# Hash attention and maxout FFN on one core: later modelled landings in the kernel's own planner, earlier weight halves, and V casts moved to GpSimd

## The chip, the core and the metric

The kernel runs on one core of a Trainium2 chip, in one launch. The metric is device time in microseconds, the median of several runs. A profiled execution of the same program gives the span, the busy times and the trace. The engines are TensorE (PE, with its weight loads as PEld), VectorE (DVE), ScalarE (ACT), GpSimd (POOL) and SyncE (SP), which here only issues transfers. Each engine works through its instructions in the order in which they stand, and waits for semaphores of the others.

## What is computed

```python
# q, k, v: (4, 8, 768, 64) fp32; proj: (64, 6)
q_bits = einsum('bhsd,dk->bhsk', q, proj) > 0     # 6 bits: a bucket
k_bits = einsum('bhsd,dk->bhsk', k, proj) > 0
scores = where(q_bucket == k_bucket, q @ k.T / 8, -1e9)
attn = softmax(scores)                            # sum + 1e-9
x = (attn @ v) laid out as (3072, 512)
h = maximum(maximum(x @ w1, x @ w2), x @ w3)      # w: (512, 768)
out = h @ w_out                                   # (3072, 512) fp32
```

A query sees only keys of its own bucket. The kernel does not mask: the bits are appended to q and k as six more rows of the contraction, with a weight so large that a key which differs in one bit vanishes in the exponential.

## The kernel before

**Tiling.** The 8 heads of each of the 4 batches are handled in pairs, so there are 16 pairs, written (b, pr) below. For one pair q, k and v are loaded by three transfers of SP (`load`, L245), into four buffers each. `split_h` and `split_r` (L259, L270) make an fp16 part and an fp16 remainder. Both are transposed, on TensorE for the first six pairs (`pe_T`, L288, evacuated by `evac_T`), and by a DMA transpose on SP for the others (`xbar`, L281). `hash_mm` (L299) multiplies by the projection; `hash_bits0` or `hash_bits` (L314, L327) compares with zero. The bits then make a trip: `bit_T` transposes them on TensorE, `bit_evac` copies them on DVE, `bit_out` (L347) writes them to DRAM and `bit_in` (L351) reads them into their rows of the operand `T`. This trip is called the bounce. Up to the third pair, `hash_mm` adds the product of the high and the low half of the projection in PSUM, by 48 matmuls; from the fourth on it makes both halves side by side by 24 matmuls, and DVE compares them by two instructions in place of one.

**V.** `vcast` (L355) casts V to fp16 into `vone`, which holds a batch and has two copies. From batch 1 on, `vsum` (L359, three GpSimd instructions) sums V over the chunks, and `mean_mm` (L368) gives the column mean by one matmul; for batch 0 it takes six matmuls of the cast V itself. The mean stands in for a query that meets no key. The cast runs on GpSimd for batches 0 and 1, and on ACT for batches 2 and 3.

**Attention.** The work of a pair is cut into 12 units, numbered through u = 0 to 191. A unit is a `score` (L389, two matmuls of 384 columns into one of two `sc` buffers), an `expo` on ACT (L399) and an `attend` (L404, six matmuls of 65 columns). Six units make a block, which has the one `av` bank until `norm_t` (L419) on DVE has read it; `norm_x` divides. All blocks of batch 0 come first (u = 0 to 47). From batch 1 on, the pairs of the first half of the queries come before those of the second: pair (1,0) starts at u = 48, (1,1) at 54, (1,2) at 60, (1,3) at 66, and (2,0) at 96.

**FFN.** When a half of a batch is normalized, `x_bar` (L456), a DMA transpose on SP, turns it. 18 `l1` (L473, four matmuls each) make six blocks of the hidden layer from three weight matrices; `l1_evac` takes the maximum on DVE, the first of three also on ACT. Three `l2` (L492, six matmuls of 512 columns) give the output rows, evacuated by `l2_evac` into `osb` buffers and sent by `store` (L504) on SP. An `l1` needs its weight half: (0,0), (0,1), (0,2) are the first halves of the three matrices, (1,0), (1,1), (1,2) the second. All six come by GpSimd transfers that cast on the way (`load_w`, L538), behind a small wait instruction `hold` (L645) for the second halves. The output weights come by SP as fp32 into two `ws` buffers (`stage_w`, L659) and are cast on GpSimd (`cast_w`, L665).

**What sets the order.** The pools, tiles and semaphores take the order of the program, and the program is written by a planner. `Plan.run` (L46) simulates the engines when the program is built: each task has an engine or a choice of two with a duration, a priority, dependencies, and counts of buffers that it takes and gives. At each modelled moment a free engine takes the ready task of the smallest priority number. A transfer is modelled as an issue on its engine, a place in one common queue for its `xfer` time, and then a fixed POST of 1.2 us until it counts as landed. The order that results is emitted; at run time each engine keeps it, however long things really take. So a change of a modelled landing changes no instruction by itself. It changes which tasks were thought ready, and thereby the order on all engines.

`mm` names three PSUM banks which `pe_T`, `hash_mm`, `bit_T`, `mean_mm`, `l1` and `l2` share, each until its evacuation.

Of the kernel before, what the change touches and what calls it, by code (L numbers as in the profile page):

```python
# [16 lines left out]


class Task:
    def __init__(self, kinds, prio, deps, emit, take=(), give=(), after=(), lat=0.0, xfer=0.0, hold=0.0):  # L20
        self.kinds, self.prio, self.emit = kinds, prio, emit
        self.deps = [d for d in deps if d is not None]
        self.take, self.give, self.lat, self.xfer, self.hold = take, give, lat, xfer, hold
        self.after = [t for t in after if t is not None]
        self.start = None


class Plan:
# [17 lines left out]
    def run(self):  # L46
        users, left = {}, {}
        for n, t in enumerate(self.tasks):
            t.n = n
            left[t] = len(t.deps)  # L50
            for d in t.deps:
                users.setdefault(d, []).append(t)
        ready = {t for t in self.tasks if not left[t]}
        engines = sorted({k[0] for t in self.tasks for k in t.kinds})
        busy = dict.fromkeys(engines, 0.0)
        queue = []
        now, events, n = 0.0, [], 0
        while n < len(self.tasks):
            moved = True
            while moved:  # L60
                moved = False
                for e in engines:
                    if busy[e] > now:
                        continue
                    best = None
                    for t in ready:
                        dur = dict(t.kinds).get(e)
                        if dur is None or any(self.free[r] <= 0 for r in t.take) or any(
                                x.start is None for x in t.after):
                            continue  # L70
                        if best is None or (t.prio, t.n) < (best[0].prio, best[0].n):
                            best = t, dur
                    if best is None:
                        if e == "PE" and self.filler and self.filler(now):
                            busy[e] = now + 0.1
                            events.append((busy[e], -1, None))
                            moved = True
                        continue
                    t, dur = best
                    ready.discard(t)  # L80
                    for r in t.take:
                        self.free[r] -= 1
                    busy[e] = now + dur
                    t.start, t.engine = now, e
                    if t.hold:
                        busy[e] = 1e9
                        events.append((now + dur, -2, t))
                    else:
                        events.append((busy[e], -1, None))
                    if t.hold:  # L90
                        pass
                    elif t.xfer:
                        events.append((busy[e] + PRE_DMA.get(e, 0.3), -2, t))
                    else:
                        events.append((now + dur + (t.lat or self.LAT[e]), t.n, t))
                    if t.emit:
                        t.emit(e)
                    n += 1
                    moved = True
            events.sort(key=lambda x: x[:2])  # L100
            if not events and not queue:
                stuck = [(t.kinds, t.prio, [r for r in t.take if self.free[r] <= 0])
                         for t in sorted(ready, key=lambda t: t.prio)]
                raise RuntimeError(f"plan stuck: {n} of {len(self.tasks)} at {now}, {self.free}: {stuck[:12]}")
            then = min(now + queue[0][0] if queue else 1e9, events[0][0] if events else 1e9)
            if queue:
                queue[0][0] -= then - now
            now = then
            while queue and queue[0][0] < 1e-6:
                t, hold = queue.pop(0)[1:]  # L110
                if hold:
                    busy[t.engine] = now
                    queue.insert(0, [t.xfer - t.hold, t, 0.0])
                    continue
                events.append((now + POST, t.n, t))
            events.sort(key=lambda x: x[:2])
            while events and events[0][0] <= now:
                at, kind, t = events.pop(0)
                if kind == -2:
                    queue.append([t.hold or t.xfer, t, t.hold])  # L120
                    continue
                if t is None:
                    continue
                for r in t.give:
                    self.free[r] += 1
                for x in users.get(t, ()):
                    left[x] -= 1
                    if not left[x]:
                        ready.add(x)
        self.end = now  # L130
# [3 lines left out]
def kernel(  # L134
# [36 lines left out]
    XT = 4  # L171
    HT = 13
    XN = 2
    OSB = 4

    konst = ctx.enter_context(tc.tile_pool(name="konst", bufs=1))
    raw = ctx.enter_context(tc.tile_pool(name="raw", bufs=4))
# [120 lines left out]

    def hash_mm(b, pr, heads, e):  # L299
        hps = bank(("h", b, pr), "hps")  # L300
        summed = 4 * b + pr < 3
        K = NBITS if summed else 2 * NBITS
        for n in range(2):
            for hh in range(*heads):
                for c in range(NCH):
                    a = n * NA2 + hh * NCH + c
                    o = hps[:, a * K : (a + 1) * K]
                    if summed:
                        for i in range(2):
                            nc.tensor.matmul(o, T[b, pr][:, a, :], PAB[:, i * K : (i + 1) * K], start=i == 0, stop=i == 1)  # L310
                    else:
                        nc.tensor.matmul(o, T[b, pr][:, a, :], PAB[:], start=True, stop=True)  # L312
# [42 lines left out]
    def vcast(b, pr, e):  # L355
        copy(e, vones[b % 2][:, 2 * pr : 2 * pr + 2, :, 0:D],
             raws["v", b, pr][:].rearrange("p h (c d) -> p h c d", d=D))
# [190 lines left out]
    def value(b, pr, dep):  # L548
        U = first_unit[b, pr]
        prev = at_last.get((b - 2, pr))  # L550
        if b == 0:
            ready_v[b, pr] = add(("POOL", 0.85), U - 6, [dep, prev], lambda e: vcast(b, pr, e), give=("v",))
            vs = ready_v[b, pr]
        else:
            ready_v[b, pr] = add(("POOL", 0.9) if b == 1 else ("ACT", 0.72), U - 6, [dep, prev], lambda e: vcast(b, pr, e))
            vs = add(("POOL", 2.0), U - 5, [dep, ready_v[b, pr], ready_m.get((b if pr > 1 else b - 1, (pr + 2) % 4))],
                     lambda e: vsum(b, pr, e), give=("v",))
        m = add(("PE", 0.34 if b == 0 else 0.06), U - 3, [vs], lambda e: mean_mm(b, pr, e), take=("mm",))
        ready_m[b, pr] = add(("DVE", 0.28), U - 3, [m], lambda e: mean_evac(b, pr, e), give=("mm",))

    def prep(b, pr):
# [3 lines left out]
        if b > 0:  # L565
            for n in "qkv":
                g = divmod(4 * b + pr - GATE, 4)
                if b == 1:
                    g = {("q", 0): (0, 2), ("k", 0): (0, 2)}.get((n, pr), (0, 3) if pr < 3 else (1, 0))
                loads[n, b, pr, (0, 2)] = add(("SP", 0.5), U - 44 + 0.1 * "qkv".index(n), [],  # L570
                                              lambda e, n=n: load(n, b, pr, (0, 2), e), take=(n,), xfer=1.1,
                                              after=[last_load[0], bounced[g], xbars.get(4 * b + pr - 2)])
                last_load[0] = loads[n, b, pr, (0, 2)]
        value(b, pr, loads["v", b, pr, (0, 2)])
# [42 lines left out]
                                  give=("mm",)))  # L617
            both_rs += rs
        if not by_pe:
            ev = [add(("SP", 0.6), p0 + 2, both_rs, lambda e: xbar(b, pr, e), xfer=4.6, hold=3.4, take=("T",))]  # L620
            xbars[4 * b + pr] = ev[0]
        plan.join(ev, ("s",))
        hm = add(("PE", 1.3 if 4 * b + pr < 3 else 0.67), p0 + 4, ev + [mp], lambda e: hash_mm(b, pr, (0, 2), e), take=("mm",))
        hb = add(("DVE", 0.3 if 4 * b + pr < 3 else 0.62), p0 + 5, [hm],
                 (lambda e: hash_bits(b, pr, e)) if 4 * b + pr >= 3 else (lambda e: hash_bits0(pr, (0, 2), e)), take=("bit",), give=("mm",))
        bT = add(("PE", 0.11), p0 + 6, [hb], lambda e: bit_T(b, pr, e), take=("mm",), give=("bit",))
        be = add(("DVE", 0.28), p0 + 6, [bT], lambda e: bit_evac(b, pr, e), take=("bt",), give=("mm",))
        bo = add(("SP", 0.65), p0 + 7, [be], lambda e: bit_out(b, pr, e), take=("dr",), give=("bt",), xfer=0.05,
                 after=[last_copy[0]])
        bi = add(("SP", 0.65), p0 + 7, [bo], lambda e: bit_in(b, pr, e), give=("dr",), xfer=0.25)  # L630
        bounced[b, pr] = last_copy[0] = bi
        if b == 0 and pr < NP - 1:
            for hh in range(2):
# [12 lines left out]
        t = small.tile([P, 1], FP16, tag="hold", name="hold")  # L646
        nc.gpsimd.tensor_copy(t[D : D + NBITS, :], T[b, pr][D : D + NBITS, NA - 1, P - 1 : P])

    plain = ()
    wst_tiles = {}  # L650

    def w_view(w, i):
# [15 lines left out]
    def weights(b, pr, parts):  # L668
        if (pr or b) and parts[0] not in plain and parts[0] != "o":
            prev = add(("POOL", 0.1), -150, [bounced[b, pr]], lambda e: hold(b, pr, e), after=[wprev[0]])  # L670
        elif pr or b:
            prev = bounced[b, pr]
        else:
            prev = ready_v[0, 1]
        for w in parts:
            if w == "o" or w in plain:
                parts = []
# [128 lines left out]
```

## Time and profile before

| | us |
|---|---|
| median of 7 runs | 274.04 |
| lowest and highest of them | 272.57, 277.96 |
| the profiled execution | 275.18 |
| its span | 273.4 |
| busy: PE, DVE, ACT, POOL | 257.9, 177.3, 196.1, 47.5 |

The profiled execution is 1.8 us longer than the span of its engines. The granted clock of TensorE was 0.999 over the span. The page's second part cuts the span into 40 slices of 6.8 us; a digit is the busy share of a slice in tenths. The engines' busy sums are union times of instructions; a matmul counts up to its modelled end, which lies after the start of the next one, so that a gap shorter than that does not show in this row.

A line of the timeline has the start, the time taken, the engine, the line of the kernel, the operation and its tiles, and in brackets how long the engine had stood idle before it and what ended that. A line of the waits has the engine, its line, what it waited for, and then the total, the number of times and the longest.

### The profile page before, as it was taken

How to read it: one execution, taken by the hardware profiler on the slowest of the kernel's cores; microseconds unless marked ns; L12 is line 12 of the kernel's file. 1: busy time of each engine (PE TensorE's matmuls, PEld its weight loads, DVE VectorE, ACT ScalarE, POOL GpSimd, SP SyncE). 2: the span in 40 equal slices, each digit the busy share in tenths (PEclk: the TensorE clock that was granted, in tenths of full speed). 3: DMA queues.
4: the chain of work that ended last, by engine and by line, in shares of the span. 5: the costliest groups of instructions: out<-in, count | busy, mean ns of one | idle time of the engine just before them, and what ended most of it. 6: DMA issues, size and time to landing. Idle time of an engine off the chain costs nothing.

```text
span 273.4 us, 7378 instructions
## 1 busy us (share of the span) xinstructions
PE 257.9 (94%) x3016; PEld 175.7 (64%) x3016; DVE 177.3 (65%) x389; ACT 196.1 (72%) x283; POOL 47.5 (17%) x61
## 2 busy tenths in 40 slices
PE   8799996699999899979999999999999999999995
PEld 8688675467656566656666667666566656555552
DVE  4898698897767698386789735565246525445250
ACT  4798997689838789868988988899889432232322
POOL 1180075753303222030330300000000000000000
PEclk9999999999999999999999999999999999999999
DMA  6996499699995979869995783300510041020303
GB/s 199 370 213 101 136 309 217 192 201 320 224 243 182 288 215 167 197 216 215 206 242 187 143 192 90 68 2 2 134 41 1 15 121 41 6 111 2 115 0 116
DMA packets 67392, 41.30 MB, mean 151 GB/s; under 512 B 48030, under 2 KB 63646, under 8 KB 67358
## 3 DMA queue, kind: packets, MB, share of 16 engines
q1 hardware_dynamic: 64110, 38.47, 54.2%
q0 software_dynamic: 3168, 2.36, 6.1%
q8 instruction: 23, 0.38, 0.6%
q14 instruction: 11, 0.09, 0.1%
q10 hardware_dynamic: 80, 0.00, 0.0%
HBM read 25.72 MB, written 6.84 MB: 119 GB/s over the span
## 4 chain that ended last, share of the span: by engine, by line
PE 71%; DMA 12%; DVE 7%; SPq 3%; POOL 2%; issue 2%; ACT 2%; ACTq 0%; POOLq 0%
PE ps L478 31%; PE sc L395 16%; PE po L496 9%; PE av L413 9%; DMA v<-in_v_dram 7%; DMA q<-in_q_dram 4%; DVE s L273 2%; SPq L250 2%; DVE s L268 2%; PE hps L312 1%; ACT AT L401 1%; PE tps L292 1%; DMA T<-dr 1%; POOL vt L363 1%; PE hps L310 1%
## 5 line engine op out<-in xcount | busy, mean ns | idle before, releaser
L401 ACT ACTIVATE AT<-sc 128x768 f16<-128x768 f32 x192 | 146.2, 812 | 20.3 <-PE sc L395 19.3
L478 PE MATMUL ps<-xT,w_sb 128*128 128x384 f16 x576 | 106.3, 326 | 0.3 <-DVE ht L204 0.3
L395 PE MATMUL sc<-T 128*128 128x384 f16 x384 | 93.2, 325 | 3.4 <-ACT AT L401 1.7
L487 DVE TENSOR_TENSOR ht<-ht,ps 128x384 f16<-128x384 f16 x96 | 53.0, 552 | 44.4 <-PE ps L478 41.0
L413 PEld LDWEIGHTS <-AT 128*128 128x128 f16 x1152 | 59.5, 97 | 23.8 <-issue 1.1
L478 PEld LDWEIGHTS <-w_sb 128*128 128x128 f16 x576 | 52.3, 98 | 29.9 <-issue 0.5
L413 PE MATMUL av<-vone,AT 128*128 128x65 f16 x1152 | 65.5, 193 | 0.5 <-DVE t L430 0.4
L395 PEld LDWEIGHTS <-T 128*128 128x128 f16 x384 | 30.5, 97 | 17.5 <-issue 5.3
L202 ACT CAST ht<-ps 128x384 f16<-128x384 f32 x32 | 15.4, 480 | 29.8 <-DVE ht L487 19.1
L496 PE MATMUL po<-wout_sb,ht 128*128 128x512 f16 (+1 forms) x150 | 33.5, 370 | 0.0
L363 POOL TENSOR_TENSOR vt<-v 128x384 f32<-128x384 f32 x12 | 14.5, 1212 | 61.1 <-DMA v<-in_v_dram 61.1
L202 ACT COPY osb<-po 128x512 f32<-128x512 f32 (+1 forms) x22 | 12.5, 566 | 17.0 <-PE po L496 17.0
L430 DVE TENSOR_TENSOR t<-av,mv 128x390 f32<-128x390 f32 x32 | 17.9, 559 | 10.3 <-PE av L413 10.3
L496 PEld LDWEIGHTS <-ht 128*128 128x128 f16 x150 | 14.2, 98 | 14.0
L273 DVE SCALAR_TENSOR_TENSOR s<-q,s 128x384 f16<-128x384 f32 x32 | 19.8, 628 | 3.3 <-ACT s L266 3.1
L273 DVE SCALAR_TENSOR_TENSOR s<-k,s 128x384 f16<-128x384 f32 x32 | 20.7, 662 | 0.1
L449 DVE TENSOR_TENSOR xn<-t,rr 128x384 f16<-128x384 f32 x32 | 19.9, 622 | 1.1
L292 PE MATMUL tps<-iden,s 128*128 128x128 f16 x168 | 14.1, 226 | 1.5 <-DVE bit L322 0.9
L292 PEld LDWEIGHTS <-s 128*128 128x128 f16 x168 | 11.0, 101 | 4.8 <-DVE mv L382 2.0
L204 DVE CAST ht<-ps 128x384 f16<-128x384 f32 x16 | 8.8, 552 | 5.7 <-PE ps L478 5.3
L204 POOL CAST vone<-v 128x768 f16<-128x768 f32 x8 | 8.3, 1041 | 16.8 <-DMA v<-in_v_dram 16.8
L204 DVE COPY T<-tps 128x768 f16<-128x768 f16 x17 | 9.2, 551 | 1.4 <-PE tps L292 1.2
(54 smaller groups left out, 151.1 us busy)
## 6 DMA issues: line engine op xcount, KB each, us to landing
v<-in_v_dram SPq DMA_DIRECT2D x16, 384.0 KB
out_dram<-osb SPq DMA_DIRECT2D x23, 256.0 KB
q<-in_q_dram SPq DMA_DIRECT2D x15, 384.0 KB
k<-in_k_dram SPq DMA_DIRECT2D x15, 384.0 KB
w_sb<-in_moe_w_dram POOLq DMA_DIRECT2D x6, 384.0 KB, 7.5
ws<-in_moe_w_out_dram SPq DMA_DIRECT2D x3, 512.0 KB
dr<-bt SPq DMA_DIRECT2D x15, 36.0 KB
T<-dr SPq DMA_DIRECT2D x15, 36.0 KB
```

What stands on the lines that cost most here:

```text
L202: nc.scalar.copy(o, i)
L204: ENG[e].tensor_copy(o, i)
L273: nc.vector.scalar_tensor_tensor(out=s[:, a0:a1, D : 2 * D], in0=raw_view(n, b, pr, heads), scalar=QS, in1=s[:, a0:a1, 0:D], op0=AluOp.mul ...
L292: nc.tensor.transpose(p16[:, c * P : (c + 1) * P], S16[b, pr][:, a0 + c, :], iden[:])
L395: nc.tensor.matmul(sc[:, i, 0:HQ], t[:, NA2 + hh * NCH + 2 * j + i, :], t[:, hh * NCH + hf * CH : hh * NCH + (hf + 1) * CH, :], start=True ...
L401: nc.scalar.activation(AT[:], scs.pop(u)[:, :, 0:HQ], ActFn.Exp, bias=EXP_BIAS, scale=EXP_SCALE)
L413: nc.tensor.matmul(av[:, o : o + D + 1], AT[:, i, c * P : (c + 1) * P], vones[b % 2][:, 2 * pr + hh, 2 * j + i, 0 : D + 1], start=slot == ...
L430: nc.vector.tensor_tensor(out=t[:, :, :, 0 : D + 1], in0=av[:, :, :, 0 : D + 1], in1=mv, op=AluOp.add)
L449: nc.vector.tensor_tensor(out=xv, in0=t[:, :, :, 0:D], in1=rr[:].to_broadcast([P, 2, CH, D]), op=AluOp.mult)
L478: nc.tensor.matmul(ps[:, 0:HQ], w_sb[i][:, jc, fb * P : (fb + 1) * P], xTs[b, hf][:, jc, :], start=jc == 0, stop=jc == NJ - 1)
L487: nc.vector.tensor_tensor(out=ht[:], in0=ht[:], in1=ps[:, 0:HQ], op=AluOp.max)
L496: nc.tensor.matmul(ps[:, m0:m1], hts[b, hf, fb][:, c * P : (c + 1) * P], wout_sb[:, fb, m0:m1], start=fb == 0, stop=fb == NF - 1)
```

## The change

- A task has a new value `pad`, which the planner adds to the landing of a transfer. DMA transposes of pairs get 4 us, q, k and v loads of pair number 4 * b + pr above 5 get 2 us, and the reading half of the bounce 3 us for the same pairs.
- Pair (0,2) uses the 24-matmul hash with the two-instruction comparison, and its modelled durations follow.
- The V cast of batches 2 and 3 is on GpSimd.
- The first weight halves wait for the V cast of (0,0) in place of that of (0,1).
- The second half of the third matrix is staged by SP as fp32 in two transfers of 384 KB and cast by two GpSimd instructions, in place of one casting GpSimd transfer with its `hold`.
- There are five `osb` buffers in place of four.

```diff
-    def __init__(self, kinds, prio, deps, emit, take=(), give=(), after=(), lat=0.0, xfer=0.0, hold=0.0):
+    def __init__(self, kinds, prio, deps, emit, take=(), give=(), after=(), lat=0.0, xfer=0.0, hold=0.0, pad=0.0):
...
-                events.append((now + POST, t.n, t))
+                events.append((now + POST + t.pad, t.n, t))
...
-    OSB = 4
+    OSB = 5
...
-        summed = 4 * b + pr < 3
+        summed = 4 * b + pr < 2
...
-            ready_v[b, pr] = add(("POOL", 0.9) if b == 1 else ("ACT", 0.72), U - 6, [dep, prev], lambda e: vcast(b, pr, e))
+            ready_v[b, pr] = add(("POOL", 0.9), U - 6, [dep, prev], lambda e: vcast(b, pr, e))
...
-                                              lambda e, n=n: load(n, b, pr, (0, 2), e), take=(n,), xfer=1.1,
+                                              lambda e, n=n: load(n, b, pr, (0, 2), e), take=(n,), xfer=1.1, pad=2 if 4 * b + pr > 5 else 0.0,
...
-            ev = [add(("SP", 0.6), p0 + 2, both_rs, lambda e: xbar(b, pr, e), xfer=4.6, hold=3.4, take=("T",))]
+            ev = [add(("SP", 0.6), p0 + 2, both_rs, lambda e: xbar(b, pr, e), pad=4, xfer=4.6, hold=3.4, take=("T",))]
...
-        bi = add(("SP", 0.65), p0 + 7, [bo], lambda e: bit_in(b, pr, e), give=("dr",), xfer=0.25)
+        bi = add(("SP", 0.65), p0 + 7, [bo], lambda e: bit_in(b, pr, e), give=("dr",), xfer=0.25, pad=3 if 4 * b + pr > 5 else 0.0)
...
-    plain = ()
+    plain = ((1, 2),)
...
-            prev = ready_v[0, 1]
+            prev = ready_v[0, 0]
```

The limits of `hash_mm`'s and `hash_bits`' modelled durations go from 3 to 2 in the same way. The order of instructions changes on all five engines. On PE it is the same up to the hash of (0,2), and the number of instructions falls by 48 (24 weight loads and 24 matmuls).

More of the change, by code (lines that the diff above doesn't have):

```diff
@@ L19 @@
 class Task:
-    def __init__(self, kinds, prio, deps, emit, take=(), give=(), after=(), lat=0.0, xfer=0.0, hold=0.0):
+    def __init__(self, kinds, prio, deps, emit, take=(), give=(), after=(), lat=0.0, xfer=0.0, hold=0.0, pad=0.0):
         self.kinds, self.prio, self.emit = kinds, prio, emit
         self.deps = [d for d in deps if d is not None]
-        self.take, self.give, self.lat, self.xfer, self.hold = take, give, lat, xfer, hold
+        self.take, self.give, self.lat, self.xfer, self.hold, self.pad = take, give, lat, xfer, hold, pad
         self.after = [t for t in after if t is not None]
@@ L619, in prep @@
         if not by_pe:
-            ev = [add(("SP", 0.6), p0 + 2, both_rs, lambda e: xbar(b, pr, e), xfer=4.6, hold=3.4, take=("T",))]
+            ev = [add(("SP", 0.6), p0 + 2, both_rs, lambda e: xbar(b, pr, e), pad=4, xfer=4.6, hold=3.4, take=("T",))]
             xbars[4 * b + pr] = ev[0]
         plan.join(ev, ("s",))
-        hm = add(("PE", 1.3 if 4 * b + pr < 3 else 0.67), p0 + 4, ev + [mp], lambda e: hash_mm(b, pr, (0, 2), e), take=("mm",))
-        hb = add(("DVE", 0.3 if 4 * b + pr < 3 else 0.62), p0 + 5, [hm],
-                 (lambda e: hash_bits(b, pr, e)) if 4 * b + pr >= 3 else (lambda e: hash_bits0(pr, (0, 2), e)), take=("bit",), give=("mm",))
+        hm = add(("PE", 1.3 if 4 * b + pr < 2 else 0.67), p0 + 4, ev + [mp], lambda e: hash_mm(b, pr, (0, 2), e), take=("mm",))
+        hb = add(("DVE", 0.3 if 4 * b + pr < 2 else 0.62), p0 + 5, [hm],
+                 (lambda e: hash_bits(b, pr, e)) if 4 * b + pr >= 2 else (lambda e: hash_bits0(pr, (0, 2), e)), take=("bit",), give=("mm",))
         bT = add(("PE", 0.11), p0 + 6, [hb], lambda e: bit_T(b, pr, e), take=("mm",), give=("bit",))
```

## The prediction

> **What bounds the kernel now.** I read the page's busy rows first, then TensorE's waits, then the timeline around each of its gaps, engine by engine back to what released it.
>
> ```profile
> span 273.4 us, 7378 instructions
> ...
> PE 257.9 (94%) x3016; PEld 175.7 (64%) x3016; DVE 177.3 (65%) x389; ACT 196.1 (72%) x283; POOL 47.5 (17%) x61
> ...
> PE   8799996699999899979999999999999999999995
> ...
> DMA  6996499699995979869995783300510041020303
> ```
>
> TensorE is the bound, at full clock. Only its gaps and its work can be gained. A busy row hides small gaps, since a matmul's modelled end lies past the start of the next, so I count start to start: a `score` takes 0.325 us of PE, an `attend` 0.19, an `l1` 0.65, an `l2` 1.295, six transposes 0.335, a hash of 24 matmuls 0.59. That gives 248.0 us of work and 17.3 us of gaps between 4.7 and 270.0 us: 4.0 in the start-up chain to 12 us, 8.0 from there to 52.2, 5.3 from there to 145, nothing after. TensorE's waits and its timeline name the large ones:
>
> ```profile
> PE svp L376 <- POOL vsum L366: 4.2, 2, 2.3
> PE sc L395 <- ACT AT L401: 1.7, 2, 1.5
> PE sc L395 <- DMA T<-dr: 1.3, 1, 1.3
> ```
>
> ```profile
> 45.41 0.22 PE L376 MATMUL svp<-vsum,ones 128*128 128x130 f16 x1 [1.91 <-POOL vsum L366]
> ...
> 52.16 0.22 PE L376 MATMUL svp<-vsum,ones 128*128 128x130 f16 x1 [2.28 <-POOL vsum L366]
> ...
> 90.91 0.50 PE L395 MATMUL sc<-T 128*128 128x384 f16 x2 [1.27 <-DMA T<-dr]
> ...
> 122.84 0.48 PE L395 MATMUL sc<-T 128*128 128x384 f16 x2 [1.52 <-ACT AT L401]
> ```
>
> Start to start these are 2.07, 2.44, 1.43 and 1.68 us. The first two are late V loads of batch 1; the third is a bounce of bits (pair 3 of batch 1); the fourth is ScalarE, stopped by a V cast whose load had not landed (next view, ScalarE and GpSimd):
>
> ```profile
> 120.76 0.83 ACT L202 CAST vone<-v 128x768 f16<-128x768 f32 x1 [1.72 <-DMA v<-in_v_dram]
> ```
>
> ```profile
> 41.65 0.95 POOL L204 CAST vone<-v 128x768 f16<-128x768 f32 x1 [0.79 <-DMA v<-in_v_dram]
> ...
> 48.22 1.17 POOL L204 CAST vone<-v 128x768 f16<-128x768 f32 x1 [2.86 <-DMA v<-in_v_dram]
> 49.35 1.30 POOL L363 TENSOR_TENSOR vt<-v 128x384 f32<-128x384 f32 x1
> ```
>
> **The change, part by part.** I use the order of instructions in the built program; (b,pr) is batch and head pair.
>
> *Hash of (0,2) in one pass.* It drops 24 matmuls: 1.18 to 0.59 us on PE. DVE pays: two instructions (304 + 307 ns) for one of 297. At 29 to 43 us the gain cannot show directly: ScalarE runs without a break there (9.98 busy of 10 in 30 to 40), and then the V loads decide. It shows through the SP queue. V of (1,0) is issued behind the bits of (0,3):
>
> ```profile
> 30.85 0.33 SPq L349 DMA_DIRECT2D dr<-bt  x1
> 32.89 0.29 SPq L352 DMA_DIRECT2D T<-dr  x1
> 33.22 0.40 SPq L250 DMA_DIRECT2D v<-in_v_dram  x1
> ```
>
> The hash of (0,3) now stands 1.10 us of PE work earlier (0.59 from the dropped matmuls, the rest because one mean and other work go behind it), and one evacuation in front of it moves from ACT to DVE. Through hash, bits, transpose and evacuation I get the bits out at about 30.0, not 30.85. The loads, the `hold` and the two weight DMAs behind it all move by 0.85, so `mean_mm` (1,2) runs at 51.3, not 52.16. Up to it PE has done 0.77 us less, of which 0.59 is work that no longer exists: 0.18 is owed. **Gain 0.67** (bounds 0 to 0.7: the V chain, not PE, is what counts here, so more is not to be had).
>
> *First weight halves sooner.* Three DMAs (0.91, 0.75, 0.75 us on GpSimd) go ahead of the V cast of (0,1). They end at 13.1; that cast starts at 13.95 anyway, when its data are there. Their packets now run from about 12.3, beside the last loads of batch 0, which share the engines (DMA 1.00 in 10 to 20) and land up to 2 to 3 us later: V of (0,3) at about 20 for 17.6. The means of (0,2) and (0,3) come at 26 to 28, so that is covered; without that cover it would cost those 2 us. The weights landed by 24 and the first `l1` is at 52.7: **0**.
>
> *Third matrix, second half, by SP and a cast.* One GpSimd DMA goes (0.78 us, at 52.5, its hold 0.40); two SP loads come directly behind the bits of (1,0), and two casts of about 1.04 (row of `wout_sb`) on GpSimd. On SP they stand ahead of q, k, v of (1,3), which land some 2.4 us later (a 393 KB load takes 1.2); the V chain of (1,3) then ends at about 60 for 58.4. Its mean stands 12.3 us of PE work behind that of (1,2), at 63.6: covered by 3 us. **0.**
>
> *A fifth output buffer.* SP's waits in front of stores name the evacuation (16 of them `osb` on ACT, 52.5 us), never a buffer: **0**.
>
> *V casts of batches 2 and 3.* ScalarE loses 8 x 0.834 = 6.7 us and the 2.3 us it waited for V. The gap at 122.84 (1.68) and the 0.29 behind it go: `mean_mm` (3,0) moves from between scores 95 and 96 to between 101 and 102. **Gain 1.97.** GpSimd gets 8 x 1.04 to 1.17 us, each ahead of its sums, so a mean is ready 1.1 later; behind each landing I find 2 to 4 us of PE work still to go, the tightest being (2,3), 2. The third cast of the output weights now stands behind cast and sums of (2,0), ending at about 76; the first `l2` is at 78: covered by 2, and a stall if the loads of (2,0) slip by more.
>
> *Padding.* It moves PE work ahead of what waits for SP. For the gap at 90.91: the last `l2` of the first half ended at 85.2, was evacuated on DVE until 87.43, and only then store (87.46) and bit load (87.91) left the in-order SP queue, landing at 90.9: 5.7 us after the `l2`, over 4.3 us of PE work. After the change 10.4 us of PE work stand there, and the evacuation is on ACT (0.59). **Gain 1.43**, with 3 us or more to spare; behind the queued bit load stand q, k, v of (2,2), whose mean has 3 us too. What is late next are the transposes, issued later on SP: the bits of (1,2), behind two of them (3.7 to 7.5 us each), land at 82.5 to 86, their score is at 86.
>
> *ScalarE and DVE jitter.* The other gaps from 98 to 145 sum to 2.2 us (scores waiting for AT, an `attend` for DVE). ScalarE, less loaded, gives back half: **gain 1.1**.
>
> *What DVE pays.* Sorted by whether GpSimd arithmetic runs beside them in the timeline, DVE instructions differ: split remainders 715 and 810 ns for 550 (29 of them), `xn` 897 for 558 (6), scalings about 940 for 560 (9), 11.6 us over 41.8 us of GpSimd work. So:
>
> ```profile
> 139.64 0.56 DVE L449 TENSOR_TENSOR xn<-t,rr 128x384 f16<-128x384 f32 x1
> 140.12 1.37 DVE L273 SCALAR_TENSOR_TENSOR s<-q,s 128x384 f16<-128x384 f32 x1
> ```
>
> Here the GpSimd sum of 139.68 to 141.07 is running. By these rows eight casts (8.9 us) add 2.5 us to DVE. The Trainium skill, "SBUF — State Buffer", section "Who interferes with whom", speaks against the change: an instruction of DVE with two SBUF inputs, or in a two-port mode, and one of GpSimd that reads SBUF exclude each other for a whole instruction. By the rule a cast costs up to its whole 1.1 us, 8.9 in all. Evacuations that read PSUM stayed at 552, as the rule has it, so only part of DVE is exposed and I take the rows. What reaches PE is a late `norm_t` (one av bank), 0.56 us as at 139.09: three hits of eight, **loss 1.7** (bounds 0 and 8.8).
>
> The sum: 0.67 + 1.97 + 1.43 + 1.1 - 1.7 = 3.5. The profiled execution took 275.18 (span 273.4 and 1.8 around it), 1.1 over the median of 274.04; against the median the forecast is 274.04 - 3.5, about **270.6**.
>
> **The rivals.**
> *DVE takes over in 52 to 75 us.* Between `norm_t` of blocks 5 and 9 DVE has 37 instructions instead of 33, since ScalarE's `l1` evacuations go to it: 17.7 us of 20.8, and 12 us of GpSimd at 0.28 add 3.3: full. PE would wait for banks by the excess and by transposes sent late, 2 to 3 us: 273.1. For it: DVE's digits 7 to 9 there. Against: in before, DVE was 24.45 busy of 32.8 and PE had no gap.
> *The padding does nothing*, bounce and score moving together: 3.5 - 1.43 less, 272.0. Against: the 10.4 us counted above.
> *Slower: the shared port.* Eight casts delay the `norm_t` before an `attend` by their full 1.1 us: 8.8 for my 1.7, 277.7. It breaks even at 5.2 us, five hits. For it: 1.37 us rows; against: blocks end 6 us apart, and a cast meets one only by chance.
>
> **How the numbers follow.** Likeliest case 0.55, by itself 268.1 (all 5.3 us of later gaps and 0.67 gone) to 272.3; DVE 0.19, padding 0.12, shared port 0.14. Within 1% (2.7 us, about what this measurement can tell from no change) lie 271.3 to 276.8: most of the DVE and padding cases. Faster 0.58, same 0.29, slower 0.13. The range, 268.1 to 275.2, leaves out the shared port case and little else.
>
> **What would show it.** Right: no wait of `sc` for `T<-dr` near 90; no ACT cast of `vone`; `svp` waits near 45 and 52 still there, the second ending near 51.3; no gap after 145. Wrong: waits of `svp` for `vsum` past 52 (GpSimd too late), `av` waiting for `t` often, `po` waiting for `wout_sb`, or a second SP wait in front of a score.

## The result, and the profile after

The changed kernel takes 271.28 us, the median of 12 runs (269.3 to 273.29), against 274.13 for 31 runs of the kernel before; the ratio is 0.9893, with a 95% interval of 0.9861 to 0.9926. That is 1.1% faster. A second submission of the same kernel gave 0.9928 (0.9888 to 0.9969). The forecast was 270.6. Some executions of every kernel take over 1.5% longer than its fastest one; the ratios and intervals leave these out, and no profile of one is read below.

The page of the profiled execution (270.41 us), its lines that answer to those shown of before:

```profile
span 268.6 us, 7323 instructions
...
PE 257.3 (96%) x2992; PEld 174.3 (65%) x2992; DVE 178.5 (66%) x390; ACT 190.7 (71%) x275; POOL 55.2 (21%) x69
...
PE   7898998799989999999999999999999999999995
...
DMA  6994599889959796996994986220230050020303
```

The span is 4.8 us shorter in this pair of profiles, more than the medians say (2.9). Counted start to start as in the prediction, PE's work fell by 0.59 and its gaps from 17.3 to 13.3 us. Of that, 0.7 lies before 12 us, where no instruction was moved: over the kernels below this stretch holds 2.6 to 5.0 us of gaps by chance, 3.3 in this profile and 5.0 in the second one of the same kernel. So I compare **the gaps after 12 us**: 13.3 before, 10.0 and 8.0 in the two profiles after.

TensorE's waits after the change (engine, line, what it waited for: total, times, longest):

```profile
PE svp L376 <- POOL vsum L366: 1.2, 1, 1.2
...
PE ps L478 <- DVE ht L487: 1.0, 3, 0.4
...
PE sc L395 <- DMA T<-dr: 0.8, 1, 0.8
PE sc L395 <- ACT AT L401: 0.6, 2, 0.4
```

The wait for V fell from 4.2 to 1.2 us (2.1 in the second profile of this kernel) and that for the exponentials from 1.7 to 0.6 (0.7). The `T<-dr` wait is another one: it stands at 26.4, at the first score of (0,1), and the one at 90.9 is gone. The wait for `ht` is larger than before. TensorE's timeline at the places of the old gaps:

```profile
49.71 0.22 PE L376 MATMUL svp<-vsum,ones 128*128 128x130 f16 x1 [1.25 <-POOL vsum L366]
...
93.66 0.65 PE L395 MATMUL sc<-T 128*128 128x384 f16 x3
...
128.48 0.22 PE L376 MATMUL svp<-vsum,ones 128*128 128x130 f16 x1
```

The first is the mean of (1,2), at 52.16 before. The second is the group with the first score of (1,3): it waits for nothing. The third is the mean of (3,0), whose sums ended at 128.16: it is just in time.

By stretch, the gaps are these (worked out afresh from the four traces, each start against the usual distance between matmuls of that shape; the sums lie up to 0.5 above those of the table further down):

| gaps of PE, us | 12 to 52.2 | 52.2 to 85 | 85 to 145 |
|---|---|---|---|
| before | 8.0 | 0.1 | 5.6 |
| changed | 7.1 | 2.5 | 0.9 |
| changed, again | 6.0 | 1.6 | 0.5 |
| before, only the padding | 7.4 | 3.9 | 0.7 |

So in both profiles of the changed kernel most of the gain is made after 85 us, and about a third to a half of that is paid back between 52 and 85.

### The profile page after: what moved, and what is told of

The parts are those of the page before. It is cut to its first block, busy times and chain, and to the rows that moved or that the text cites. A ratio compares the mean times of both kernels' runs of the same rounds, so it can differ in the third digit from the quotient of the medians.

```text
span 268.6 us, 7323 instructions
## 1 busy us (share of the span) xinstructions
PE 257.3 (96%) x2992; PEld 174.3 (65%) x2992; DVE 178.5 (66%) x390; ACT 190.7 (71%) x275; POOL 55.2 (21%) x69
## 3 DMA queue, kind: packets, MB, share of 16 engines
q0 software_dynamic: 2640, 1.97, 4.8%
## 4 chain that ended last, share of the span: by engine, by line
PE 76%; DMA 8%; DVE 7%; issue 2%; ACT 2%; SPq 2%; POOL 1%; ACTq 0%; POOLq 0%
PE ps L478 32%; PE sc L395 18%; PE po L496 12%; PE av L413 10%; DMA v<-in_v_dram 4%; PE hps L312 3%; DVE s L273 2%; DMA q<-in_q_dram 2%; SPq L250 2%; DMA dr<-bt 2%; ACT AT L401 1%; DVE ht L487 1%; DVE s L268 1%; DMA T<-dr 1%; DVE T L204 1%
## 5 line engine op out<-in xcount | busy, mean ns | idle before, releaser
L478 PEld LDWEIGHTS <-w_sb 128*128 128x128 f16 x576 | 52.2, 98 | 31.9 <-issue 2.7
L395 PEld LDWEIGHTS <-T 128*128 128x128 f16 x384 | 30.4, 97 | 14.4 <-issue 3.1
L204 POOL CAST vone<-v 128x768 f16<-128x768 f32 x16 | 13.8, 863 | 81.2 <-DMA v<-in_v_dram 58.0
L202 ACT COPY osb<-po 128x512 f32<-128x512 f32 (+1 forms) x24 | 13.6, 568 | 17.9 <-PE po L496 17.7
L273 DVE SCALAR_TENSOR_TENSOR s<-q,s 128x384 f16<-128x384 f32 x32 | 21.9, 701 | 4.5 <-ACT s L266 4.5
L449 DVE TENSOR_TENSOR xn<-t,rr 128x384 f16<-128x384 f32 x32 | 20.9, 654 | 1.1
L273 DVE SCALAR_TENSOR_TENSOR s<-k,s 128x384 f16<-128x384 f32 x32 | 19.4, 625 | 0.6 <-ACT s L266 0.5
L204 DVE CAST ht<-ps 128x384 f16<-128x384 f32 x17 | 9.4, 554 | 8.8 <-PE ps L478 8.8
L292 PE MATMUL tps<-iden,s 128*128 128x128 f16 x168 | 13.4, 220 | 1.7 <-DVE s L273 0.9
L312 PEld LDWEIGHTS <-T 128*128 128x128 f16 x336 | 10.0, 96 | 1.0
```

What stands on the lines that cost most here:

```text
L202: nc.scalar.copy(o, i)
L204: ENG[e].tensor_copy(o, i)
L273: nc.vector.scalar_tensor_tensor(out=s[:, a0:a1, D : 2 * D], in0=raw_view(n, b, pr, heads), scalar=QS, in1=s[:, a0:a1, 0:D], op0=AluOp.mul ...
L292: nc.tensor.transpose(p16[:, c * P : (c + 1) * P], S16[b, pr][:, a0 + c, :], iden[:])
L395: nc.tensor.matmul(sc[:, i, 0:HQ], t[:, NA2 + hh * NCH + 2 * j + i, :], t[:, hh * NCH + hf * CH : hh * NCH + (hf + 1) * CH, :], start=True ...
L449: nc.vector.tensor_tensor(out=xv, in0=t[:, :, :, 0:D], in1=rr[:].to_broadcast([P, 2, CH, D]), op=AluOp.mult)
```

## The experiments

To tell the parts apart although every one of them reshuffles the planner's order, some kernels keep the order of one kernel and change only what is emitted ("order kept"); the others let the planner make a new one. Each column of gaps is of one profile, and these differ by 1 to 2 us between executions of one kernel, as the two of the changed kernel show; a dash stands where no profile is read. Ratios are to the kernel before on the same chip.

| kernel | ratio (95%) | PE gaps after 12 us |
|---|---|---|
| changed | 0.9893 (0.9861 to 0.9926) | 10.0 |
| changed, again | 0.9928 (0.9888 to 0.9969) | 8.0 |
| before, order kept, V cast on GpSimd | 0.9977 (0.9925 to 1.003) | 15.0 |
| before, order kept, hash of (0,2) in one pass | 0.9948 (0.9912 to 0.9984) | 12.3 |
| before, only the padding | 0.9889 (0.9848 to 0.9931) | 12.0 |
| changed without the padding | 0.9997 (0.9951 to 1.0042) | 11.5 |
| changed, first weights late again | 0.992 (0.988 to 0.996) | - |
| changed, third matrix by GpSimd again | 0.9932 (0.9898 to 0.9966) | 12.7 |
| changed, order kept, V cast on ScalarE | 0.9839 (0.9799 to 0.988), again 0.993 (0.9888 to 0.9971) | 10.8, 9.7 |
| changed, order kept, one cast on ScalarE | 0.9919 (0.9879 to 0.996) | - |
| changed, order kept, casts twice | 1.0045 (0.9998 to 1.0092) | 11.8 |
| changed, V cast on ScalarE in the plan too | 0.9889 (0.9842 to 0.9936) | 8.9 |

**The V cast alone, in the old order.**

```diff
     def vcast(b, pr, e):
-        copy(e, vones[b % 2][:, 2 * pr : 2 * pr + 2, :, 0:D],
+        copy("POOL", vones[b % 2][:, 2 * pr : 2 * pr + 2, :, 0:D],
```

> The order of before, unchanged, with only the V cast of batches 2 and 3 on GpSimd instead of ScalarE. My theory (the cast on ScalarE held up the exponentials when V was late): the 1.68 us gap of a score near 122.8 goes, and time falls by 1.5 to 2 us, since PE's order is that of before and the bounce near 90 (1.4 us) stays. Rival (the gain of the whole change comes from the new order, and GpSimd pays DVE back through the shared port): 0 to 1 us slower than before, with DVE busy up by 2 us or more.

0.9977 is not to be told from no change, and its interval (2.1 us faster to 0.8 slower) excludes neither theory by time. DVE is busy 179.0 us against 177.3, near the 2 us of the rival. The timelines of GpSimd and TensorE of this kernel show why:

```profile
121.15 1.13 POOL L204 CAST vone<-v 128x768 f16<-128x768 f32 x1 [13.91 <-DMA v<-in_v_dram]
122.25 1.33 POOL L363 TENSOR_TENSOR vt<-v 128x384 f32<-128x384 f32 x1
...
124.38 0.46 POOL L366 TENSOR_TENSOR vsum<-vt,vt 128x128 f16<-128x128 f32 x1
```

```profile
124.89 0.22 PE L376 MATMUL svp<-vsum,ones 128*128 128x130 f16 x1 [1.94 <-POOL vsum L366]
```

The exponentials no longer wait, as forecast. But the mean of (3,0) stands 0.8 us of PE work behind that score in this order, and its sums now follow the cast on the same engine: PE waits 1.94 us for them, in place of the 1.5 it waited for the exponential. One late load was handed from one wait to the other. (The gap of 1.4 at the bounce near 92 stayed, and a 2.0 us wait for a transpose near 62 is of this profile alone.)

**The same cast, the other way round, in the new order.** The edit is `copy("ACT" if b > 1 else e, ...)`.

> The order of the changed kernel, unchanged, with only the V cast of batches 2 and 3 back on ScalarE. If the cast on ScalarE is what cost 2 us, it comes back: 2 us over the changed kernel. If the planner's order now leaves ScalarE slack and the cast on GpSimd only stretches DVE (PE gaps near 70 to 76, 2.0 us in all), the time is equal or up to 1.5 us lower than that of the changed kernel, and those gaps shrink.

> The order of the changed kernel with the V casts of batches 2 and 3 on ScalarE, a second time. If the first reading (0.984 of before) holds, the casts on GpSimd cost the changed kernel (0.989 and 0.993 of before) about 0.7% net; if it was chance, it is at 0.989 to 0.993.

The two readings, 0.984 and 0.993, lie on both sides of the changed kernel's; the interval of the first does not reach that of the second, so these intervals are narrower than what comes between two submissions. Together they say: not slower than the changed kernel. The first theory (2 us come back) is refuted. The profiles, of one PE order, show what the casts do to DVE: it is busy 175.2 and 173.5 us with the casts on ScalarE, 178.5 and 177.0 with them on GpSimd. The mean difference is 3.4 us, for 8 casts of some 0.86. Two other pairs show less: 1.7 us in the old order (the run above), and 1.6 us for eight more casts (the doubled ones below, 179.3). So 1.6 to 3.4 us. The second theory is met only in part: PE's gaps from 52 to 85 are 1.9 and 1.3 us here, against 2.5 and 1.6 with the casts on GpSimd, so most of them have another cause than the casts.

**And with an order made for it.** The planner's line for batches 2 and 3 is set back to ScalarE, all else as changed.

> The changed kernel with the V casts of batches 2 and 3 on ScalarE for the planner too, so with an order made for it. If the padding carries the gain: 0.5 to 1.5% under before, like the changed kernel. If the move of the cast is needed: within 0.4% of before, with an exponential waiting behind a cast for V.

0.9889, with the lowest median of all (269.59 of 6 runs) and 8.9 us of gaps. So the gain does not need the move of the cast. Its sums there end 1.8 to 6.4 us ahead of the means of (2,1) to (3,2), and 0.7 ahead of (3,3). That it beats the changed kernel is not shown: the intervals overlap.

**Padding alone.** The diff's `pad` lines on the kernel before.

> Before with only the padding of modelled landings (a new order on all engines, nothing else). My theory (padding puts PE work in front of what waits for SP): the wait of a score for T<-dr near 90 goes, 1 to 1.5 us are gained, and the V waits near 45 and 52 stay. Rival (a later modelled landing only reshuffles, and the waits move elsewhere): the sum of PE's gaps after 52 us stays at 5 us or more, and the time within 1 us of before.

0.9889: **the padding by itself gives as much as the whole change**, by the time. Its profile is one of the longer executions of this kernel (273.67, the median is 272.24), and shows 1.3 us less of gaps than before. The gap at 90 went (a wait for `T<-dr` of 0.7 is left, elsewhere), and from 85 us to 213 only two gaps of over 0.2 us are left, 0.44 and 0.26, where before had 5.3 us. New ones stand from 52 to 85 us, about 4 us, mostly PE behind DVE. Of the V waits near 45 and 52, which were to stay, one of 1.0 us is left, but the gaps up to 52 us are nearly those of before: waits of other kinds took their place. Which of the three paddings does it (transposes, loads or read-backs), and whether other amounts would do as well, was not tried.

**All but padding.** The landing event of the changed kernel without `+ t.pad`.

> The changed kernel without the padding of modelled landings, so with another order, and all else as changed. If padding carries the gain after 52 us, the time goes back to within 0.5% of before less the hash's 0.5%: 1.5 to 2.5 us over the changed kernel, with waits of svp for vsum or of sc for T<-dr after 85 us. Rival (hash, weights and casts carry it): within 0.7 us of the changed kernel.

0.9997 (0.9951 to 1.0042): without padding no gain shows, although the one-pass hash is in this kernel too. TensorE's waits of this kernel name what padding had removed:

```profile
PE svp L376 <- POOL vsum L366: 3.7, 5, 1.2
...
PE sc L395 <- DMA T<-dr: 0.9, 1, 0.9
```

Five means wait for V instead of one or two, the later ones at 119.4 (0.73) and 138.8 (0.31). The expected size, 1.5 to 2.5 us over the changed kernel, is met: by the two ratios on the same chip it is 1.9. That a chance reshuffle and not the padding makes the difference is unlikely by the table: apart from the doubled casts, the kernels with padding, of five different plans, lie between 0.984 and 0.993, and the three without it between 0.995 and 1.000.

**Hash alone, in the old order.** The limits of `hash_mm` and `hash_bits` are set to 2, and the planner keeps its durations.

> The order of before, unchanged, with only the hash of pair (0,2) in one pass of 24 matmuls. If the saved 0.59 us of PE work goes through the bounce of (0,3) to the V loads of batch 1, both svp waits near 45 and 52 end about 0.6 earlier and the time falls by 0.5 us. If DVE's extra instruction or ScalarE, full there, eats it: no change.

0.9948, or 1.4 us (0.4 to 2.4): the 0.5 expected lies in it. But the traces do not show the way that was worked out. The bits of (0,3) leave at 30.04 here and at 29.81 in the changed kernel, against 30.85 before (SP of this kernel, then of the changed one):

```profile
30.04 0.32 SPq L349 DMA_DIRECT2D dr<-bt  x1
33.60 0.29 SPq L352 DMA_DIRECT2D T<-dr  x1
```

```profile
29.81 0.32 SPq L349 DMA_DIRECT2D dr<-bt  x1
31.49 0.29 SPq L352 DMA_DIRECT2D T<-dr  x1
```

In the second profile of the changed kernel, though, they leave no earlier than before, and with the old hash and the V casts on GpSimd they leave earlier than in any of these (first of the one, then of the other):

```profile
30.86 0.33 SPq L349 DMA_DIRECT2D dr<-bt  x1
```

```profile
29.71 0.33 SPq L349 DMA_DIRECT2D dr<-bt  x1
```

So this moment varies by as much between executions as the hash was to move it. The read back starts 3.56 us after the write here, 1.68 in the changed kernel, and 2.04 before. The gap of the mean of (1,1) stayed, 2.07; that of (1,2) fell from 2.44 to 0.15, but two gaps of 0.66 and 0.52 stand beside it, and the sum of gaps up to 52 us is 8.1, as before (8.0). Of the two waits only that of (1,2) ended earlier. Where the 1.4 us come from stays open.

**First weights, and the staging.** `prev = ready_v[0, 1]`, and `plain = ()`, each in the changed kernel.

> The changed kernel with the first weight halves behind the V cast of (0,1) again. My theory: these weights have 25 us to spare, so their own landing is worth 0; what changes is the planner's order, so within 1 us of the changed kernel, either way. Rival (their early landing frees the transfers of 16 to 24 us and hurries the bounces): 1 us or more over the changed kernel, with the bits of (0,1) to (0,3) later.

> The changed kernel with the second half of the third matrix by a casting GpSimd transfer again, behind its hold. My theory: covered either way, within 1 us of the changed kernel. Rival (the two SP loads and two casts delay q, k, v of (1,3) and lengthen DVE near 50): 1 us or more faster without them.

0.992 and 0.9932 beside 0.9928: neither is worth anything that shows, as forecast.

**One cast moved, and all casts doubled.** `"ACT" if (b, pr) == (2, 0) else e`; and for the doubling the cast in a loop of two for batches 2 and 3, which writes the same values again.

> The order of the changed kernel with only the cast of (2,0) on ScalarE, which idles 1.7 and 2.8 us there. If the shared port is what stretches DVE between 68 and 74 us, the PE gaps from 70 to 77 (2.0 us in the profile) fall below 1 us and the time falls by about 1 us; if DVE's longer list is the cause, they stay.

> The order of the changed kernel with each V cast of batches 2 and 3 done twice on GpSimd (8 times 0.86 us more, the result the same). By the shares seen before, DVE gets 2 us longer. If the means have only 0.3 to 0.9 us to spare behind the sums, as the trace of the changed kernel shows at (2,1), (2,3) and (3,0), PE waits of svp for vsum appear after 85 us and the time rises by 1.5 to 4 us; if the padding left 2 to 4 us, as forecast, nothing happens beyond the DVE part, under 1 us.

One cast: 0.9919, no difference in time that shows, so the first expectation (1 us) is not confirmed; no profile of it is read, and whether the gaps from 70 to 77 fall stays open. Doubling: 1.0045, 1.2 to 1.5% over the changed kernel's two ratios, for 7 to 8 us of GpSimd work. That is over 3 us of end time. The gaps of its profile, 1.8 us above the mean of the first and 3.8 above the second of the changed kernel, fit; they stand where forecast only in part: PE behind DVE at 74 to 77 (1.8 us) and at 101.9 (0.85), one mean at 110.4 (0.43). In the time, GpSimd has little slack to give away here; the traces place only a part of the loss (PE's waits for V after 85 us are one of 0.26), and the rest was not found.

## Why the prediction was right, point by point

- **Size and sign**: 270.6 forecast, 271.28 measured. The sum is right partly by luck: the gain counted with the cast belongs to the padding, and the loss counted with the casts came by another way.
- **The hash (0.67)**: the hash alone measures 1.4 us with an interval that holds 0.67, but its way is not shown. Mean (1,2) came at 49.71, not the 51.3 worked out, behind bits that left 1.04 earlier. In the second profile it came at 49.86 without a wait, behind bits that left at 30.86; there the mean of (1,1) waited (second profile):

```profile
45.57 0.22 PE L376 MATMUL svp<-vsum,ones 128*128 128x130 f16 x1 [1.84 <-POOL vsum L366]
```

  So of the sign "waits near 45 and 52 still there" each profile shows one.
- **First weights, staging: 0**. Confirmed by undoing each. That the fifth output buffer is worth 0 was not tried.
- **"V casts of batches 2 and 3. Gain 1.97" failed.** The step took away a wait of ScalarE and placed the 1.97 with the cast. In the old order no gain from the cast's move shows (0.9977), and its trace has the mean behind the same load waiting; in the new order the gain is there with the cast on either engine. Padding alone, with the cast on ScalarE, has no gap above 0.44 us from 85 us on; without padding the mean of (3,0) waits again. So it is the later place of the mean in a padded plan that removes the gap. I had named that place in a clause and counted the gain under the wrong part.
- **Padding (1.43): right mechanism, too small.** It alone is worth 3.0 us (1.9 to 4.2). The bounce behaved as worked out: the `l2` ended at 83.28, ScalarE evacuated it, the store left at 84.36. The bit load left only at 89.12, 5.2 us after the bits' own write, which had been issued at 83.91 right behind loads of (2,1); that these held it up is likely but not shown. Its score ran at 93.66 without a wait.
- **"Behind each landing I find 2 to 4 us of PE work": too optimistic.** The sums of (2,1), (2,3) and (3,0) end 0.9, 0.6 and 0.3 us ahead of their means (1.0, 1.2 and 1.2 in the second profile, where the mean of (2,0) waited 0.27 behind a cast of 2.35 us: a sign of being wrong that I had named). I counted cast and sums at their unhindered durations; `vsum` of (2,1), for one, took 3.65 us instead of 2.5. The time of the doubled casts fits a slack that is gone; their trace shows it at one mean.
- **Jitter (1.1)**: of the 2.2 us, in which the 0.29 that stands with the cast is by its own sums counted again, less than half is left: from 85 to 145 us the gaps of all kinds are 0.9 and 0.5. The reason, a less loaded ScalarE, is not borne out: padding alone, with the casts on ScalarE, has 0.7 there.
- **What DVE pays (1.7)**: eight casts made DVE 1.6 to 3.4 us longer, for 2.5 forecast from the rows and 8.9 by the full exclusive rule; the measurement stands nearer to the rows. The way to PE was another one. No `norm_t` made an `attend` wait in the first profile, and one did for 0.3 us in the second; the cast and sums of (2,0), with the last cast of the output weights, ran beside DVE from 68.3 to 73.2 (DVE, changed kernel):

```profile
68.36 1.17 DVE L449 TENSOR_TENSOR xn<-t,rr 128x384 f16<-128x384 f32 x1
...
69.65 1.90 DVE L273 SCALAR_TENSOR_TENSOR s<-q,s 128x384 f16<-128x384 f32 x2
71.48 0.81 DVE L268 TENSOR_SCALAR s<-k 128x768 f16<-128x768 f32 x1
...
72.67 0.92 DVE L273 SCALAR_TENSOR_TENSOR s<-k,s 128x384 f16<-128x384 f32 x1
```

  Against 0.56, 1.02 for the two, 0.56 and 0.55 these are 2.1 us longer, and the `l1` behind waited for banks: 1.95 us of gaps from 70 to 76.3. This is the place of the first rival (DVE in 52 to 75), and partly its mechanism, at a price under its 2 to 3 us. Most of it is not the casts: with them on ScalarE in the same order the gaps from 52 to 85 us fall only from 2.5 and 1.6 to 1.9 and 1.3, and padding alone has 3.9. How much of the rest is the sums on GpSimd and how much DVE's longer list was not separated.
- **The padding rival** ("bounce and score moving together") is refuted by padding alone. **The shared-port rival** did not come at eight casts. Sixteen did take the whole gain, but not by the rival's way: DVE grew by 1.6 us, and no wait of an `attend` for DVE is in that profile's list.

## What to carry to other kernels

When an order is made by a modelled schedule, later modelled landings for what the hardware delivers irregularly can be worth more than moving work between engines, as here. A wait that is taken away from one engine has to be followed to the next user of the same late data, in the same order of instructions. And a gain should be credited to a part only after that part was run alone with the order kept, since any edit to a planner's input reshuffles the rest.

## What the runs showed of the hardware

The trip of a bounce, from the issue of the write to the issue of the read, was 1.68, 2.04 and 3.56 us for the same bits of (0,3) in three kernels, and 1.91 in another execution of the one with 1.68; what sets it was not found. The first 12 us, the same instructions in all kernels on PE, held between 2.6 and 5.0 us of PE gaps. And a GpSimd cast of the same shape ran in 0.82 us at best, in 1.13 to 1.17 at other times, and once in 2.35.
